# dK/dV as quarter-height row tiles, with fixed PSUM banks and a new step order, in a two-layer decode backward pass

## The chip, the cores and the metric

The kernel runs on one core of a Trainium2 chip. The metric is device time in microseconds (us). Each run of an experiment alternates with runs of the kernel before on the same chip. A ratio below is the mean time of one kernel's fast runs over the mean of the other's fast runs in the same rounds, so it is not quite the ratio of the medians quoted beside it. A run counts as fast when it is at most 1.5% above the fastest of the same kernel. Intervals are at 95%.

PE is the TensorE (matrix engine), PEld its weight loads, DVE and ACT the two engines that copy results out of PSUM (the banks into which the products are written), POOL the engine that issues the stores, SP the one that issues the loads. The granted clock is TensorE's clock as a share of full speed.

## The reference, cut to what matters

```python
# A: attention of one query token per batch over a cache, 32 query heads on 4 KV heads
q = (x @ wq) ...                        # B=2, D=1024, Hq=32, Hkv=4, Sk=16384, Dh=128
p = softmax(q k^T * Dh**-0.5); o = p v; A = o @ wo
# B: MLP with layernorm, gelu; D=1024, F=3584
x = x + A(ln(x)); x = x + B(ln(x)); x = x + A(ln(x)); x = x + B(ln(x))
# returned: the output, and the gradients of x, k_cache, v_cache, wq, wo, w1, b1, w2, b2
```

Both attention layers use the same caches. The gradients of K and V are therefore sums over two layers and eight query heads: for each of 8 groups (batch x KV head) and each cache row, 16 coefficients times 16 vectors of 128.

## The kernel before

The last stage walks through 32 chunks of 32 columns t (128 cache rows each), two "steps" of 16 columns per chunk. A step transposes V, makes the scores of dP, dS from them, accumulates dQ with K, makes dV and dK, and takes some "fill" units: the weight gradients, 512 columns each.

PSUM is shared out by pools; `px` is a pool of four banks for everything that is a matrix product here:

```python
ps_x = ctx.enter_context(tc.tile_pool(name="ps_x", bufs=4, space=PSUM))
def px(shape, dtype, name):
    return ps_x.tile(shape, dtype, name=name, tag="x")
```

dK/dV: for each of two t quads (a = 0 and 1), 64 coefficients (2 layers l x 8 heads x 4 t) against a block-diagonal matrix of 64 x (4 t x 128 d). Each quad is a row tile, half of the array's height:

```python
def kv_block(w, i, b):
    ...
    for a in range(2):
        ps = px([128, 4, 128], F32, "kv_ps")
        PE.matmul(ps[:]..., lhsT=blk[64 * a:64 * a + 64, b, :], rhs=Qm[64 * a:64 * a + 64, :, :]...,
                  start=True, stop=True, tile_position=(64 * a, 0))
        pss.append(ps)
    for a in range(2):
        evac_cast(sv_[:, b * 8 + a * 4:b * 8 + a * 4 + 4, :], pss[a][:], 512)
```

The backward product of Wq comes in four quarters. Its sum is kept in one tile of the same pool, from the first push of a quarter to the last:

```python
def quarter(kv):
    ...
    if j0 == 0 and j == 0:
        box["ps"] = px([128, DJ, 2], F32, "dn_b")           # one of the four banks, held
        V.memset(box["ps"][:], 0.0)
        box["pipe"] = BwdPipe(box["ps"], dq_all[:, hs, 0:2], True)
    ...
    box["pipe"].push(box["wv"], j, j0 + j, 0, 8)            # 8 transposes, a copy, 8 matmuls into dn_b
    if j0 + j == DJ - 1:
        box["pipe"].flush()
        V.tensor_tensor(out=dn_acc[:], in0=dn_acc[:], in1=box["ps"][:], op=ALU.add)
```

The step, cut to its order:

```python
while 2 * m < NS + 12 or late or fill:
    for s in (2 * m, 2 * m + 1):  kTs[s] = emit_T(cv, b, False)      # V transposes
    ... make_blk_V(i)                                                # on even m
    for s in (2 * m - 2, 2 * m - 1):  score0(s)
    kv_step(m, 0)                       # dV: 2 banks, dK: 2 banks
    sch.run_slot(1)                     # dQ accumulation
    ... make_blk_K(m // 2 - 2)
    step_fill((5 if m < 8 else 3) if m > 0 else 1)     # late (Wq) first, then the other weights
    kv_step(m, 1)                       # dV: 2 banks, dK: 2 banks
    m += 1
```

## Time and profile before

Median 1318.79 us of 3 runs (1310.5 to 1321.18); the profiled execution spans 1303.9 us.

These lines are from the page of the kernel before: busy time, share of the span and number of instructions of each engine, then the granted TensorE clock and the busy share of the DMA engines in 40 slices, in tenths.

```profile
PE 1108.1 (85%) x17053; PEld 801.8 (61%) x17053; DVE 631.0 (48%) x1320; ACT 573.0 (44%) x1407; POOL 63.5 (5%) x113
...
PEclk9998875879889589998998986795559657866655
DMA  9999999999999899999976827897779877978846
```

The last 17 slices look different from the rest: lower clock, DMA no longer full. The windows view puts numbers to it. Its columns are the stretch and its length in us, the busy us of PE, PEld, DVE, ACT and POOL with their instructions, the mean granted clock, the DMA share and GB/s. The stretches are: a piece of the first attention; all before the last stage; the last stage; its middle (60 us after its start to the last V transpose); and its tail.

```profile
60.00:140.00 80.00, 68.28 (x1209) 55.37 (x1206) 36.14 (x76) 35.18 (x156) 0.00 (x0) 0.91 1.01 425
0.00:757.70 757.70, 622.77 (x12528) 542.09 (x12528) 297.92 (x708) 263.85 (x837) 6.04 (x15) 0.86 0.95 383
757.70:1303.90 546.20, 485.35 (x4532) 259.72 (x4528) 333.09 (x612) 309.10 (x570) 57.48 (x98) 0.66 0.78 303
817.70:1230.30 412.60, 369.00 (x3569) 200.46 (x3567) 249.80 (x460) 233.20 (x432) 41.66 (x74) 0.67 0.85 330
1230.30:1303.90 73.60, 62.74 (x382) 27.13 (x379) 43.84 (x78) 39.31 (x70) 10.74 (x16) 0.57 0.57 235
```

For 757.7 us DMA is busy 0.95 of the time. The last stage takes 546.2 us; there no engine looks full but PE (485 us), and the clock is 0.66.

The next fence is the timeline of PE within one step of the stretch in which Wq's quarter is on its way (start, us, engine, line, operation, out<-in, shape, count, and in brackets PE's idle time before it and what ended it).

```profile
905.16 0.58 PE L831 MATMUL kv_ps<-QmK,blkK 64*128 64x512 bf16 x1 [0.25 <-ACT kv_stgV L150]
905.67 0.62 PE L338 MATMUL acc<-kv_K,dS_17826 128*32 128x512 bf16 x4
...
907.18 1.03 PE L245 MATMUL wtp<-ident,wqt 128*128 128x128 bf16 x8
908.01 0.40 PE L256 MATMUL dn_b<-dq_all,wT 128*128 128x2 bf16 x8
908.34 0.60 PE L734 MATMUL dw_ps<-rowsA,rowsB 4*128 4x512 bf16 x1
908.88 0.61 PE L831 MATMUL kv_ps<-QmV,blkV 64*128 64x512 bf16 x2
909.62 1.15 PE L831 MATMUL kv_ps<-QmK,blkK 64*128 64x512 bf16 x2
910.70 1.89 PE L317 MATMUL tp<-ident,kv_V 128*128 128x128 bf16 x16
912.38 0.62 PE L892 MATMUL dp<-doT_bf_16038,kT 128*128 128x8 bf16 x16
912.93 0.61 PE L831 MATMUL kv_ps<-QmV,blkV 64*128 64x512 bf16 x2
913.34 0.63 PE L831 MATMUL kv_ps<-QmK,blkK 64*128 64x512 bf16 x1
914.21 0.58 PE L831 MATMUL kv_ps<-QmK,blkK 64*128 64x512 bf16 x1 [0.25 <-ACT kv_stgV L150]
```

A step takes 9.05 us here (905.16 to 914.21). Two dK/dV matmuls of a pair that run side by side take 0.61 us together; the pair at 909.62 took 1.15, and at 913.34 and 914.21 the second one starts 0.87 us after the first: it waited for its bank to be copied out. The tile view of `dn_b` for this quarter (count, shortest/median/longest ns, first and last start):

```profile
L256 PE MATMUL dn_b<-dq_all,wT x64: 165/165/212, 898.4 to 956.4; 128*128 128x2 bf16 x64
L861 DVE MEMSET dn_b<- x1: 72/72/72, 889.8 to 889.8; 128x16 f32 x1
L870 DVE TENSOR_TENSOR dn_acc<-dn_acc,dn_b x1: 172/172/172, 956.6 to 956.6; 128x16 f32<-128x16 f32 x1
```

### The profile page before, as it was taken

Reading aid. Unit: us, or ns where it says so; the run is one execution under the profiler, and the core shown is the slowest. Engines: PE = TensorE matmul, PEld = TensorE weight load, DVE = VectorE, ACT = ScalarE, POOL = GpSimd, SP = SyncE. Lnnn points to the kernel's source line nnn. Section 1 sums busy time; section 2 is a strip of 40 time slices with the busy share of each in tenths; the row PEclk is TensorE's granted clock in tenths of the full one; section 3 lists DMA queues with packets and bytes.
Section 4 is the critical chain, followed back from the end, with each engine's and each line's share of the span. In section 5 each row is a group of like instructions: output and inputs, shape, how many; then the busy total and the mean of one; then the engine's idle time right before and its main releaser. Section 6 shows DMA issues by size and latency. Waiting matters only on the chain.

```text
span 1303.9 us, 38655 instructions
## 1 busy us (share of the span) xinstructions
PE 1108.1 (85%) x17053; PEld 801.8 (61%) x17053; DVE 631.0 (48%) x1320; ACT 573.0 (44%) x1407; POOL 63.5 (5%) x113
## 2 busy tenths in 40 slices
PE   4989874888988589878989989889998898898997
PEld 4867654876776579767789964445454545444442
DVE  1544421334444154433344556684457556655656
ACT  0544330234445024433333456674457455654655
POOL 0000000000000000000000001110011001000112
PEclk9998875879889589998998986795559657866655
DMA  9999999999999899999976827897779877978846
GB/s 379 423 425 424 424 417 395 347 397 426 419 424 399 320 396 343 424 424 425 425 271 230 309 99 260 334 410 284 282 282 415 350 304 311 408 271 317 325 195 257
DMA packets 86916, 455.51 MB, mean 349 GB/s; under 512 B 7122, under 2 KB 7122, under 8 KB 45788
## 3 DMA queue, kind: packets, MB, share of 16 engines
q1 hardware_dynamic: 69996, 354.46, 68.3%
q0 software_dynamic: 16752, 98.59, 18.7%
q8 instruction: 133, 2.18, 0.6%
q14 instruction: 35, 0.29, 0.1%
HBM read 354.44 MB, written 98.58 MB: 347 GB/s over the span
## 4 chain that ended last, share of the span: by engine, by line
PE 60%; DMA 24%; ACT 7%; DVE 6%; issue 2%; POOL 0%; SPq 0%; POOLq 0%; DVEq 0%; ACTq 0%
PE tp L317 15%; DMA kv_V<-in_A_v_cache_dram 13%; PE wtp L245 10%; PE kv_ps L831 7%; PE dw_ps L734 5%; PE acc L338 5%; DMA kv_K<-in_A_k_cache_dram 4%; DMA wt<-in_A_wo_dram 3%; ACT kv_stgV L150 2%; PE sc L452 2%; PE o_ps L349 2%; PE dp L892 2%; ACT dw_stg L150 2%; DMA wt<-in_B_w_dram 1%; DVE kT L145 1%
## 5 line engine op out<-in xcount | busy, mean ns | idle before, releaser
L142 ACT COPY kT<-tp 128x512 int32<-128x512 int32 x273 | 159.9, 586 | 343.7 <-PE tp L317 331.5
L145 DVE COPY kT<-tp 128x1024 bf16<-128x1024 bf16 x239 | 163.7, 690 | 210.7 <-PE tp L317 202.0
L317 PE MATMUL tp<-ident,kv_V 128*128 128x128 bf16 x2048 | 184.2, 253 | 12.4 <-DMA kv_V<-in_A_v_cache_dram 12.3
L317 PEld LDWEIGHTS <-kv_V 128*128 128x128 bf16 x2048 | 149.1, 115 | 60.1 <-issue 46.8
L317 PE MATMUL tp<-ident,kv_K 128*128 128x128 bf16 x2048 | 170.8, 232 | 5.1 <-DMA kv_K<-in_A_k_cache_dram 5.1
L245 PE MATMUL wtp<-ident,wt 128*128 128x128 bf16 x1664 | 137.9, 232 | 3.1 <-issue 1.7
L317 PEld LDWEIGHTS <-kv_K 128*128 128x128 bf16 x2048 | 129.1, 103 | 5.9 <-DMA kv_K<-in_A_k_cache_dram 5.7
L142 ACT COPY wT<-wtp 128x512 int32<-128x512 int32 x126 | 72.9, 579 | 136.1 <-PE wtp L245 116.4
L145 DVE COPY wT<-wtp 128x1024 bf16<-128x1024 bf16 x122 | 80.7, 665 | 105.3 <-PE wtp L245 104.8
L150 ACT CAST kv_stgV<-kv_ps 128x512 bf16<-128x512 f32 x164 | 92.7, 587 | 47.8 <-PE kv_ps L831 46.8
L831 PE MATMUL kv_ps<-QmK,blkK 64*128 64x512 bf16 x256 | 99.8, 502 | 15.1 <-ACT kv_stgV L150 4.9
L245 PEld LDWEIGHTS <-wt 128*128 128x128 bf16 x1664 | 106.2, 104 | 3.9 <-issue 2.4
L153 DVE CAST dw_stg<-dw_ps 128x512 bf16<-128x512 f32 x112 | 75.7, 688 | 40.4 <-PE dw_ps L734 39.3
L452 PEld LDWEIGHTS <-kT 128*128 128x128 bf16 x2048 | 76.7, 98 | 28.8 <-issue 21.2
L150 ACT CAST dw_stg<-dw_ps 128x512 bf16<-128x512 f32 x128 | 72.3, 591 | 43.8 <-PE dw_ps L734 42.7
L150 ACT CAST kv_stgK<-kv_ps 128x512 bf16<-128x512 f32 x137 | 80.2, 591 | 17.9 <-PE kv_ps L831 16.9
L153 DVE CAST kv_stgK<-kv_ps 128x512 bf16<-128x512 f32 x119 | 81.3, 685 | 12.5 <-PE kv_ps L831 10.1
L279 PEld LDWEIGHTS <-wt 128*128 128x128 bf16 x1920 | 54.3, 103 | 48.0 <-DMA wt<-in_A_wo_dram 14.0
L338 PE MATMUL acc<-kv_V,e_all 128*32 128x512 bf16 x512 | 56.3, 446 | 29.8 <-DMA kv_V<-in_A_v_cache_dram 24.7
L256 PEld LDWEIGHTS <-wT 128*128 128x128 bf16 x1920 | 77.2, 99 | 7.1 <-DVE wT L145 4.8
L153 DVE CAST kv_stgV<-kv_ps 128x512 bf16<-128x512 f32 x92 | 63.3, 688 | 35.9 <-PE kv_ps L831 35.1
L831 PE MATMUL kv_ps<-QmV,blkV 64*128 64x512 bf16 x256 | 75.8, 493 | 3.3 <-DVE dw_stg L153 1.0
(561 smaller groups left out, 1392.5 us busy)
## 6 DMA issues: line engine op xcount, KB each, us to landing
kv_K<-in_A_k_cache_dram SPq DMA_DIRECT2D x116, 1024.0 KB, 9.9
kv_V<-in_A_v_cache_dram SPq DMA_DIRECT2D x116, 1024.0 KB, 10.4
wt<-in_A_wo_dram SPq DMA_DIRECT2D x32, 1024.0 KB, 8.9
out_dram<-kv_stgV POOLq DMA_DIRECT2D x32, 1024.0 KB, 6.9
out_dram<-kv_stgK POOLq DMA_DIRECT2D x32, 1024.0 KB, 10.8
wt<-in_B_w_dram SPq DMA_DIRECT2D x32, 896.0 KB, 12.0
wt<-in_A_wq_dram SPq DMA_DIRECT2D x24, 1024.0 KB, 8.2
out_dram<-dw_stg POOLq DMA_DIRECT2D x23, 1024.0 KB, 5.4
```

The source lines that it names most:

```text
L142: S.copy(out=dst.bitcast(I32), in_=src.bitcast(I32))
L145: V.tensor_copy(out=dst, in_=src)
L150: S.copy(out=dst, in_=src)
L153: V.tensor_copy(out=dst, in_=src)
L245: PE.transpose(tp[:, o, :], wv[:, j, (o0 + o) * 128:(o0 + o + 1) * 128], ident[:])
L256: PE.matmul(self.out_ps[:, jj, :], lhsT=wT[:, o, :], rhs=self.gT[:, o0 + o, :], start=False, stop=True, skip_group_check=True)
L279: PE.matmul(fps[:, jo, :], lhsT=wv[:, j, jo * 128:(jo + 1) * 128], rhs=xT_bf[:, j0 + j, :], start=False, stop=True, skip_group_check=True)
L317: PE.transpose(tp[:, j, :], cv[:, b * 8 + j, :], ident[:])
L338: PE.matmul(self.acc[32 * cg:32 * cg + 32, :], lhsT=self.coef(b4), rhs=self.cv[:, q * 16 + cg * 4:q * 16 + cg * 4 + 4, :].rearrange("p t d ...
L452: PE.matmul(sc[g][f][:, :, t % TH], lhsT=kT[:, j, :], rhs=q_bf[:, g, :], start=True, stop=True)
L734: PE.matmul(ps[:], lhsT=xrows[p:p + 4, (j0 + j) * 128:(j0 + j + 1) * 128], rhs=yrows[p:p + 4, y0 + c0:y0 + c0 + 512], start=True, stop=Tru ...
L831: PE.matmul(ps[:].rearrange("p a b -> p (a b)"), lhsT=blk[64 * a:64 * a + 64, b, :], rhs=Qm[64 * a:64 * a + 64, :, :].rearrange("p a b -> ...
```

## The change

Its intent is to make the dK/dV products cheaper on TensorE and to take the waits for PSUM out of the last stage. Coefficients are laid out by t pair, not t quad, so 32 of them (2 layers x 8 heads x 2 t) form a row tile of a quarter of the array's height, and four run side by side. The same layout goes into the accumulations of O and dQ (128x16 weights against 256 columns, sixteen per chunk instead of eight). The four banks and the two transpose banks are fixed tiles in rotation; stores rotate over the eight tiles that held the last group's K and V; Wq's product of a push goes into any bank and is added to its sum at once; V's and K's coefficients are transposed and copied together; fill is four units per step, taken in turn from two queues.

```diff
-        pss = []
-        for a in range(2):
-            ps = px([128, 4, 128], F32, "kv_ps")
-            PE.matmul(ps[:]..., lhsT=blk[64 * a:64 * a + 64, b, :], rhs=Qm[64 * a:64 * a + 64, :, :]...,
-                      start=True, stop=True, tile_position=(64 * a, 0))
+        pss = [mx() for _ in range(4)]
+        for b in range(2):
+            for r in range(4):
+                PE.matmul(pss[r][:, b * 256:(b + 1) * 256], lhsT=blk[32 * r:32 * r + 32, o + 2 * h + b, :],
+                          rhs=Qm[32 * r:32 * r + 32, :, :]..., start=True, stop=True, tile_position=(32 * r, 0))
+        for r in range(4):
+            evac_cast(sv_[:, 2 * h:2 * h + 2, r], pss[r][:]..., 512)
...
-                        box["ps"] = px([128, DJ, 2], F32, "dn_b")
+        def product(wT, j):
+            ps = mx()
+            for o in range(8):
+                PE.matmul(ps[:, 0:2], lhsT=wT[:, o, :], rhs=dq_all[:, kv * 8 + o, 0:2], start=(o == 0), stop=(o == 7))
+            V.tensor_tensor(out=dn_acc[:, j, :], in0=dn_acc[:, j, :], in1=ps[:, 0:2], op=ALU.add)
...
     def step_fill(n):
-        for _ in range(n):
-            if late: late.popleft()()
-            elif fill: fill.popleft()()
+        for k in range(n):
+            for q in ((late, fill) if k % 2 == 0 else (fill, late)):
+                if q and q[0].ready():
+                    q.popleft()()
+                    break
...
+        for k in range(2):                  # the step: one slot, then the other
+            s = 2 * m + k
+            ... transposes of slot s; score0(s - 2)
+            if k == 1 and late_pe: late_pe.popleft()()          # Wq
+            ... make_blks(m // 2, m // 2 - 2)                   # V and K coefficients together
+            kv_step("KV"[k], m, (5, 1)[k])                      # four banks
         sch.run_slot(1)
-        step_fill((5 if m < 8 else 3) if m > 0 else 1)
-        kv_step(m, 1)
+        step_fill((5 if m < 8 else 4) if m > 0 else 1)
```

## The prediction

> **What bounds it now.** The windows view cuts the kernel in two. Up to about 755 us it reads caches and weights: DMA share 0.95, TensorE clock 0.86. DMA binds, and little should change there. From 755 to 1304 us (549 us) dK/dV and the weight gradients are made: DMA share only 0.78, PE busy 488 of 549 us, DVE 334, ACT 310, granted clock 0.66. So TensorE, at half clock much of the time, binds this stage. Inside it the timeline shows two regimes. At full clock (975 to 1005 us: clock 0.95, DMA share 1.01) a step of two slots takes about 5.4 us, DMA-bound. While Wq's backward runs (889 to 982 us: clock 0.54) a step takes about 9 us, and the TensorE is busy 86 of 93 us. The last 54 us are mostly weight-gradient work (clock 0.50, DMA share 0.53).
>
> **What the change does there.**
> - dK/dV products: 512 matmuls 64x512, two row tiles at once, become 1024 of 32x256, four at once. Before's pairs start together (timeline). Per step the streamed time halves: four pairs of about 0.43 us at half clock become half of that, so -0.85 us (-0.43 us at full clock). The Trainium skill, "TensorE: Matmul & The Clock Gate", Part 3, measures 3.07x for four 32-row tiles, so most of it should arrive.
> - Waits for PSUM: in a 9 us step the dK/dV products take 3.6 us from start to next start, against 1.7 us of streaming. One of the four rotating banks is held by Wq's accumulator for a whole quarter. The change frees it and spaces the uses four at a time between transposes. I expect -0.5 to -1 us.
> - dK coefficients: 16 small transposes per chunk become 4, and two 128x512 copies become one 128x1024: -0.1 us per step.
> - Fill: four units a step, not three, alternating between jobs in different row tiles, so their matmuls overlap. The tail mostly vanishes (-25 to -35 us); per step +0.6 us of evictions and 0.13 MB of stores.
> - Acc: twice as many matmuls, half as wide, half-width eviction: neutral.
>
> **Floor.** The stage moves 303 GB/s x 549 us = 166 MB; at the 424 GB/s seen earlier that is 392 us. Evictions are about 15 per step at 0.64 us on two engines, plus 0.9 us of DVE work: about 5.3 us a step. TensorE at half clock needs about 6 us. Three limits near 6 us do not overlap perfectly: I take 6.5 us x 65 steps = 423 us, plus 45 us of start and end = 468 us. Saving about 80 us in the profile (1304 to about 1222). The skill's same page, Part 4, says transposes do not count as busy for the clock; so fewer products may leave the clock at half, which is why I don't take the whole way to the floor.
>
> **Prediction:** 1225 us, 8 in 10 within 1170 to 1275; faster by over 2% 0.93, within 2% 0.05, slower 0.02.
>
> **What would show it.** Right: the stage after 755 us shrinks to 430 to 500 us with DMA share above 0.85; the dK/dV matmuls start four at once; Wq steps fall from 9 to below 7.5 us; the tail falls below 30 us; the first 755 us stay within 10 us. Wrong: steps stay at 9 us with PE waiting for DVE/ACT evictions (four banks asked for at once), or the granted clock falls below 0.6 and eats the saving, or stores wait for homes (DMA waits in front of dK/dV evictions), or the first stage grows through the doubled accumulation matmuls. If the clock rises to 0.8 or more, the stage reaches its DMA floor and the time goes to about 1160 us.

## More of the kernel before

From 889.8 to 956.6 us one of the four banks holds sixteen numbers per partition. In that stretch the clock is at half throughout:

```profile
889.00:957.00 68.00, 62.74 (x517) 32.28 (x516) 32.96 (x56) 31.24 (x56) 5.02 (x9) 0.50 0.73 273
```

PE counts as busy for 62.74 of 68 us, and that reading is treacherous: a matmul that is slow because of the clock counts as busy in full. Over this whole profile a dK/dV matmul takes 604 ns (median) at half clock and 372 ns at full clock.

## The result, and the profile after

Median 1224.06 us of 3 runs (1223.42 to 1226.32) against 1318.79 us; the ratio is 0.93 (0.9233 to 0.9366). The profiled execution spans 1222.2 us.

The page's busy line, and the windows of the kernel after, cut as for before:

```profile
PE 1016.8 (83%) x18045; PEld 784.8 (64%) x18045; DVE 612.2 (50%) x1298; ACT 558.7 (46%) x1396; POOL 76.8 (6%) x145
```

```profile
60.00:140.00 80.00, 63.75 (x1267) 52.00 (x1267) 34.05 (x71) 32.87 (x153) 0.00 (x0) 0.92 1.01 419
0.00:766.90 766.90, 613.59 (x13198) 537.86 (x13199) 295.77 (x710) 261.21 (x836) 6.82 (x17) 0.86 0.95 379
766.90:1222.20 455.30, 403.23 (x4853) 246.92 (x4850) 316.45 (x588) 297.50 (x560) 69.95 (x128) 0.65 0.90 362
826.90:1175.00 348.10, 319.64 (x3897) 197.95 (x3897) 253.95 (x463) 241.79 (x456) 59.69 (x110) 0.64 1.00 405
1175.00:1222.20 47.20, 32.91 (x290) 16.59 (x287) 22.29 (x51) 17.81 (x34) 4.47 (x8) 0.54 0.67 271
```

The last stage is 90.9 us shorter (546.2 to 455.3): 64.5 us in its middle, 26.4 us in its tail. The middle is now at DMA share 1.00. The clock is not higher (0.65 against 0.66). The first stage is 9.2 us longer, and its reads run at 419, not 425 GB/s. 90.9 - 9.2 = 81.7 us is the difference of the spans.

The timeline of PE shows the quarter-height products of one half step of the kernel after:

```profile
986.28 0.41 PE L922 MATMUL dp<-doT_bf_16728,kT 128*128 128x8 bf16 x8
986.62 0.39 PE L858 MATMUL xm_16741<-QmK,blk 32*128 32x256 bf16 x1
986.62 0.39 PE L858 MATMUL xm_16738<-QmK,blk 32*128 32x256 bf16 x1
986.63 0.39 PE L858 MATMUL xm_16739<-QmK,blk 32*128 32x256 bf16 x1
986.63 0.39 PE L858 MATMUL xm_16740<-QmK,blk 32*128 32x256 bf16 x1
986.81 0.42 PE L858 MATMUL xm_16741<-QmK,blk 32*128 32x256 bf16 x1
...
987.17 1.03 PE L988 MATMUL tpm_16743<-ident,kv_V 128*128 128x128 bf16 x8
```

The four start within 0.01 us of each other, the next four 0.19 us later, and the next transposes start 0.55 us after the group does (986.62 to 987.17). By the picture alone, the row tiles do what they are meant to do, and the total lies 1 us from the forecast.

### The profile page after: what moved, and what is told of

It reads as the page before. It is cut to its first block, busy times and chain, and to the rows that moved or that the text cites. A ratio compares the mean times of both kernels' runs of the same rounds, so it can differ in the third digit from the quotient of the medians.

```text
span 1222.2 us, 40886 instructions
## 1 busy us (share of the span) xinstructions
PE 1016.8 (83%) x18045; PEld 784.8 (64%) x18045; DVE 612.2 (50%) x1298; ACT 558.7 (46%) x1396; POOL 76.8 (6%) x145
## 5 line engine op out<-in xcount | busy, mean ns | idle before, releaser
L144 ACT COPY kT<-tp 128x512 int32<-128x512 int32 x200 | 117.5, 588 | 286.0 <-PE tp L316 276.3
L144 ACT COPY wT<-wtp 128x512 int32<-128x512 int32 (+1 forms) x109 | 63.2, 580 | 122.1 <-PE wtp L247 112.6
L147 DVE COPY wT<-wtp 128x1024 bf16<-128x1024 bf16 (+1 forms) x107 | 70.3, 659 | 91.8 <-PE wtp L247 88.0
L452 PEld LDWEIGHTS <-kT 128*128 128x128 bf16 x2048 | 76.3, 98 | 27.3 <-issue 20.5
L316 PE MATMUL tp<-ident,kv_V 128*128 128x128 bf16 x896 | 74.4, 231 | 9.7 <-DMA kv_V<-in_A_v_cache_dram 8.9
L416 ACT ACTIVATE e_all<-sc,negm 128x64 bf16<-128x64 f32 x256 | 77.2, 345 | 1.4 <-DVE negm L411 1.4
L336 PE MATMUL acc_all<-kv_V,e_all 128*16 128x256 bf16 x896 | 47.2, 290 | 27.0 <-DMA kv_V<-in_A_v_cache_dram 24.8
L416 ACT ACTIVATION_READ_ACCUMULATOR e_all<-sc,negm 128x1 f32 x256 | 60.3, 236 | 0.0
L988 PE MATMUL tpm_16742<-ident,kv_V 128*128 128x128 bf16 x448 | 50.9, 283 | 0.0
L988 PE MATMUL tpm_16743<-ident,kv_V 128*128 128x128 bf16 x448 | 49.6, 278 | 0.0
L922 PE MATMUL dp<-doT_bf_16728,kT 128*128 128x8 bf16 x1024 | 49.5, 176 | 0.0
L922 PEld LDWEIGHTS <-kT 128*128 128x128 bf16 x1024 | 48.2, 109 | 0.4 <-issue 0.4
```

Source lines behind the costliest of these rows:

```text
L144: S.copy(out=dst.bitcast(I32), in_=src.bitcast(I32))
L147: V.tensor_copy(out=dst, in_=src)
L316: PE.transpose(tp[:, j, :], cv[:, b * 8 + j, :], ident[:])
L336: PE.matmul(ACCT[cg:cg + 16, 0:256], lhsT=self.coef(u), rhs=self.cv[:, t:t + 2, :].rearrange("p t d -> p (t d)"), start=(u < 4), stop=(u > ...
L416: S.activation(out=e_all[:, g, f * half:(f + 1) * half, l, h, :], in_=sc[g][f][:, h, :].rearrange("p (a b) -> p a b", b=2), func=ACT.Exp, ...
L452: PE.matmul(sc[g][f][:, :, t % TH], lhsT=kT[:, j, :], rhs=q_bf[:, g, :], start=True, stop=True)
```

## The experiments

Three theories. R: TensorE's streaming at half clock bound the last stage, and halving it is the main gain. B: waits for PSUM banks bound it, above all the bank held for Wq. S: the gain comes from the fill rate and the shorter tail. Names with `a_` start from the kernel after, with `b_` from the kernel before. All runs gave correct results.

| run | what differs | median us | before us | ratio (95%) |
|---|---|---|---|---|
| a_half | after, 64-row tiles | 1214.53 | 1305.09 | 0.9314 (0.9265 to 0.9363) |
| a_fill3 | after, three fill units | 1227.92 | 1305.09 | 0.9404 (0.9339 to 0.9469) |
| b_fill4 | before, four fill units | 1310.46 | 1305.09 | 1.0023 (0.9954 to 1.0092) |
| b_bank | before, bank freed | 1263.98 | 1305.09 | 0.9692 (0.9636 to 0.9749) |
| a_again | after, unchanged | 1229.16 | 1310.77 | 0.938 (0.935 to 0.9411) |
| a_pad | after, 64 bytes of padding | 1218.21 | 1310.77 | 0.9301 (0.9264 to 0.9338) |
| a_hold | a_half, bank held again | 1283.96 | 1310.77 | 0.9791 (0.9755 to 0.9827) |
| b_bank4 | b_bank, four fill units | 1272.76 | 1310.77 | 0.9699 (0.9654 to 0.9745) |
| b_space4 | b_bank4, step order of after | 1231.23 | 1307.74 | 0.9443 (0.9394 to 0.9492) |
| a_halfpad | a_half and a_pad | 1206.63 | 1307.74 | 0.9242 (0.92 to 0.9283) |
| a_best | a_halfpad, last Wq quarter transposed ahead | 1211.8 | 1307.74 | 0.9294 (0.926 to 0.9328) |
| a_halfold | a_halfpad, fill queues as before | 1208.02 | 1306.35 | 0.9248 (0.9201 to 0.9295) |

Runs with equal "before" values shared a call.

### a_half: are the row tiles the gain?

```diff
-                PE.matmul(pss[r][:, b * 256:(b + 1) * 256], lhsT=blk[32 * r:32 * r + 32, ...], rhs=Qm[32 * r:32 * r + 32]...)
+                PE.matmul(pss[2 * b + a][:], lhsT=blk[64 * a:64 * a + 64, ...], rhs=Qm[64 * a:64 * a + 64]...)   # Qm is 4 x 128 wide
```

> The kernel after, with only the dK/dV products put back to 64-row tiles (512 matmuls of 64x512, two at once) and their stationary operand widened to match; coefficients by t pair, bank and home rotation, order and fill stay. Theory R (row tiles: TensorE streaming at half clock was what bound the last stage, so halving it is the main gain): the products cost 0.85 us more per step at half clock, 0.43 us at full clock, over 64 steps, so 30 to 55 us come back, 1255 to 1280 us. Theory S (scheduling: bank rotation, spacing, fill, tail): under 12 us come back, at most 1236 us.

It took 1214.53 us, ratio 0.9314: with tiles of half the height, and twice the streaming, the whole gain is still there. Theory R falls for the kernel after, where the middle of the stage is at its DMA rate with either tile. No run puts quarter tiles alone into the kernel before, so what they would have been worth there, with the bank still held, is not shown. Windows of its last stage, whole and middle:

```profile
770.50:1217.50 447.00, 379.05 (x4370) 213.09 (x4366) 315.71 (x591) 295.66 (x557) 69.99 (x128) 0.80 0.90 368
830.50:1172.00 341.50, 296.14 (x3508) 165.44 (x3507) 255.08 (x468) 242.06 (x457) 59.89 (x110) 0.83 1.01 413
```

PE is busy for less time than with quarter tiles (379.05 against 403.23 us), although its tiles stream twice the columns; the clock is 0.80 and not 0.65. The clock records of both have the values 0.5 and 1.0 alone, as the Trainium skill says ("TensorE: Matmul & The Clock Gate", Part 1: two states, set by how busy the array has been). In the last stage they give half clock for 176 of 447.0 us with 64-row tiles, and 323 of 455.3 us with 32-row tiles. What the quarter tiles saved in columns they lost in clock. That the form of the dK/dV products is the cause is shown, since the edit changes only them, their operand and the order in which their results are copied out. That it acts by a lower activity of the array is the page's mechanism, and fits, but no run measures the activity itself.

The prediction said that at a clock of 0.8 or more the time would go to about 1160 us. Here the clock is 0.80 and it does not: the stage takes 447.0 us, with its middle at DMA share 1.01.

### b_bank and a_hold: the held bank

b_bank gives the kernel before what `product` of the change does, and nothing else:

```diff
-                        box["ps"] = px([128, DJ, 2], F32, "dn_b")      # held through a quarter
+            ps = px([128, 2], F32, "dn_b")                             # one push, then
+            V.tensor_tensor(out=dn_acc[:, jj, :], in0=dn_acc[:, jj, :], in1=ps[:], op=ALU.add)
```

> The kernel before, with Wq's product given a bank per push and added to its sum by DVE, so that no PSUM bank is held through a quarter. If the held bank was what made the dK/dV products wait in the 9 us steps (3.6 us from start to start for 1.7 us of streaming), those steps fall to 8 to 8.5 us, 32 of them, 16 to 32 us faster than before. If the waits come from two evictions engines being behind whatever the number of banks: within 8 us of before.

The ratio is 0.9692, beyond the range that even the theory of the bank gave. The window of b_bank is a Wq stretch like the one shown of before, then the whole last stage:

```profile
898.00:958.00 60.00, 53.61 (x628) 31.24 (x616) 38.78 (x76) 36.14 (x69) 5.33 (x10) 0.76 0.88 342
760.90:1262.30 501.40, 444.49 (x4532) 246.35 (x4528) 332.82 (x636) 307.02 (x570) 57.67 (x98) 0.72 0.84 330
```

The matmuls are the same in number (x4532). In the first Wq quarter the pushes start 9.33 us apart before (888.97 to 954.30 us, seven gaps) and 6.50 us apart here (899.23 to 944.75), and the clock there is 0.76, not 0.50. So the low clock before was in good part a result of the waits, not their cause. The gain also lies where the bank was held: over the three quarters of Wq that fall among the steps, the pushes span 183.8 us before and 136.8 us in b_bank, 47.0 us less, and the last stage is 44.8 us shorter.

a_hold does the opposite. It takes a_half, holds bank 3 for Wq's sum while a quarter is on its way, and lets the rest rotate over three (dK/dV go two and two, since four banks are no longer there):

```diff
-        return nxt("x", X)
+        return nxt("x", X[:3] if late_pe else X)
...
-            ps = mx()
+            ps = X[3][:, 0:2 * DJ]...        # added to dn_acc once, after the last push
```

> The kernel after with 64-row tiles (as a_half), and Wq's sum again held in one of the four banks while a quarter of Wq is on the way, the other uses rotating over three. Theory B (the held bank was the main loss before): 25 to 45 us slower than a_half's 0.931 of before, 0.95 to 0.966. Rival (order and spacing alone make up for it): below 0.940.

It gave 0.9791: of the 0.0686 that a_half gains, 0.0477 is lost, about 62 us, more than expected. Over the same three quarters its pushes span 211.6 us, a_half's 142.3: 69.3 us more, where its last stage is 68.3 us longer. Theory B is confirmed from both sides. Its last stage:

```profile
768.50:1283.80 515.30, 458.27 (x4373) 237.38 (x4370) 320.37 (x563) 301.34 (x557) 69.97 (x128) 0.66 0.82 319
```

The clock is back at 0.66, at nearly the same number of matmuls as a_half (x4373 and x4370).

The Trainium skill says that consistent bubbles can mean there is too little PSUM for the next tile ("Perfetto Trace Analysis", Optimization Strategy). The bracket [0.25 <-ACT kv_stgV L150] recurs at 905.16 and 914.21, one step apart. But the brackets alone undersize it; most of the cost is hidden in matmuls that count as busy.

### b_fill4, b_bank4, a_fill3: fill rate and tail

```diff
-        step_fill((5 if m < 8 else 3) if m > 0 else 1)
+        step_fill((5 if m < 8 else 4) if m > 0 else 1)      # b_fill4; b_bank4 with b_bank; a_fill3 the reverse
```

> The kernel before, with four fill units per step instead of three. Theory S: the tail of 54 us mostly goes, 25 to 40 us faster than before. Theory R: the steps lengthen by nearly what the tail loses, since TensorE at half clock binds them: within 12 us of before.

> The kernel before with the freed bank and four fill units. b_fill4 alone gave nothing, b_bank alone 0.969. If the missing fill rate counts only once the bank is free (the steps then have room, the tail of 73 us after the last V transposes goes to about 48): 12 to 25 us faster than b_bank, 0.950 to 0.960. If the stage is by then bound by bytes or by waits that need the new spacing: within 8 us of b_bank.

> The kernel after, with three fill units per step instead of four (60 instead of about none of the weight-gradient matmuls fall after the last V transposes). Theory D (the stage is now at its DMA rate, 420 GB/s from 820 to 1190 us): steps get shorter by about what they no longer store, the same bytes move later, a tail with idle DMA of 10 to 20 us appears, 1230 to 1245 us. Theory S: the fill rate and the missing tail are the main gain: 1255 us or more. Theory R alone: about 1224 to 1235 us.

b_fill4 is 1.0023 of before, b_bank4 0.9699 against b_bank's 0.9692, a_fill3 0.9404 where a_again has 0.938. The fill rate is worth nothing measurable in any of the three. (b_fill4's profile fell in a slower execution and is not used.) Theory S, as far as fill goes, falls: the tail of 73.6 us before is cut to 47.2 us after, but the same evictions and stores then stand in the steps. So it is in b_bank4 against b_bank: the tail falls from 73.5 to 51.5 us, and the middle grows from 367.9 to 395.8 us (here the latter):

```profile
823.30:1219.10 395.80, 351.55 (x3652) 198.14 (x3650) 266.43 (x501) 245.00 (x462) 46.87 (x80) 0.72 0.92 359
```

b_bank4 missed its expectation of a further 12 to 25 us; a_fill3, expected at 1230 to 1245 us, came out just below, at 1227.92.

### b_space4: the order of the step

```diff
-        for s in (2 * m, 2 * m + 1):  ... emit_T ...       # both slots
-        for s in (2 * m - 2, 2 * m - 1):  ... score0 ...
-        kv_step(m, 0) ; run_slot ; step_fill ; kv_step(m, 1)
+        for k in range(2):  emit_T(2m+k) ; score0(2m+k-2) ; kv_step(m, k)
+        run_slot ; step_fill
```

> b_bank4 with one thing more: the step's order is that of the kernel after (transposes of a slot, its scores, then one group of dK/dV products, twice; then accumulation and fill), so that no two groups of bank users stand next to each other but the fill. b_bank4 was 0.970 of before, the kernel after 0.938 with the same 64-byte offset undone 0.930. Theory B2 (banks: a group of four evictions needs TensorE work without a bank beside it): 0.935 to 0.950, DMA share in the middle of the stage from 0.92 to 0.97 or more. Rival (the rest comes from the merged coefficient transposes, alternating fill, quarter tiles): 0.962 or more.

The ratio goes from 0.9699 to 0.9443, as the theory of banks said. Middle of its last stage, with 64-row tiles and every other part of before:

```profile
821.00:1176.90 355.90, 325.49 (x3656) 186.49 (x3656) 260.00 (x491) 240.40 (x469) 46.58 (x80) 0.76 0.97 394
```

The DMA share there is 0.97, where b_bank4 had 0.92 (its middle: 395.8 us). Order alone, with no instruction taken away, brought the stage nearly to its DMA rate. That it acts through the banks shows in the pairs of dK/dV matmuls: in the middle of the stage the second starts over 0.1 us after the first in 101 of 214 pairs before, in 64 of 214 in b_bank4, and in 31 of 214 here. A group of bank users did better with work beside it that uses none.

### a_again and a_pad: the slower reads

The profiles of the kernel before and of its variants show 425 GB/s from 60 to 140 us, the kernel after and a_half 419. By the memory map of the compiled programs, the load buffers are at address 74496 before (a multiple of 256) and at 74432 after (64 below). a_pad adds 64 bytes:

```diff
+    pad = const.tile([128, 16], F32, name="pad")
+    V.memset(pad[:], 0.0)
```

> The kernel after, unchanged, as the control for the others of this call: ratio 0.925 to 0.937 to before; first stage again at 418 to 420 GB/s, where all kernels of the before family showed 425.

> The kernel after with 64 bytes of padding among the constants, so that the load buffers start at the same SBUF address as before (74496, a multiple of 256) and not 64 bytes lower. Theory A (the start address of the load buffers sets the DMA rate): the first stage goes back to 424 to 426 GB/s and ends 7 to 11 us earlier, 0.991 to 0.995 of a_again. Rival (the slower reads come from the doubled accumulation matmuls, or from the narrower writes of exp): rate stays at 418 to 420, time within 3 us of a_again.

a_pad took 1218.21 us, a_again 1229.16 us in the same rounds: 0.991. (a_again's 0.938 lies just outside its expected 0.925 to 0.937.) The window 60 to 140 us, of a_again and then of a_pad:

```profile
60.00:140.00 80.00, 64.73 (x1272) 53.09 (x1272) 34.26 (x72) 33.25 (x154) 0.00 (x0) 0.90 1.01 418
```

```profile
60.00:140.00 80.00, 67.68 (x1297) 54.98 (x1290) 34.75 (x73) 34.08 (x155) 0.00 (x0) 0.87 1.01 424
```

The DMA share is 1.01 in both: DMA is as busy, and moves less. The last stage starts at 765.6 us in a_again and at 758.9 us in a_pad. (a_pad's profiled execution was its slowest, 1228.25 us; the others lie between 1214.87 and 1222.07.) So the 64 bytes are the cause; they move everything allocated behind them, and that it is the load buffers that matter is likely but not separated. The Trainium skill has a possible reason ("DMA: Bandwidth & Descriptors", How a descriptor splits into AXI transactions): a transaction that reads must start at a 256-byte boundary, and a descriptor that does not begin there costs extra beats. The page says this of reads, while here the shifted address is the one that the loads write to. If its rule held for that side too, a run of 8192 bytes that starts 192 past a boundary would need 262 beats instead of 256, an estimate of 2.3%; measured is 1.4%. No run shows the beats.

### a_halfpad, a_best, a_halfold: a better version, and what is left

> 64-row tiles (a_half) and the 64-byte padding (a_pad) together. The two are independent (the first stage gains 7 to 11 us from the reads; the last stage is at its DMA rate either way): 0.922 to 0.929 of before; a_pad with quarter tiles was 0.930. Granted clock of the last stage about 0.80 against 0.62 with quarter tiles.

a_halfpad is 0.9242 of before, the fastest of all, 1206.63 us; a_pad, the same with quarter tiles, had 0.9301. Its last stage and the middle of it:

```profile
758.20:1204.60 446.40, 376.19 (x4372) 213.20 (x4368) 315.78 (x591) 295.22 (x557) 69.82 (x128) 0.81 0.90 369
818.20:1160.50 342.30, 294.06 (x3496) 166.36 (x3495) 254.18 (x466) 240.89 (x455) 59.74 (x110) 0.84 1.00 411
```

a_best tried to shorten the tail by transposing the last Wq quarter before its dQ is there, into the space of e_all of groups already done:

```diff
+        if len(ready) == G - 2:
+            make_ahead(HKV - 2)      # load, 8 x 8 transposes, copies into e_all[:, 0:2] and e_all[:, 4:6]
```

> a_halfpad, and for the last quarter of Wq the transposes are made ahead, into the space of coefficients no longer needed, since they don't wait for dQ; after dQ only the products are left. The tail from the last V transposes to the end is 45.5 us in a_half, of which about 24 us are nine steps of transpose, copy, product one after the other: 10 to 15 us less, 0.912 to 0.921 of before. If the tail is bound by its stores instead: no change from a_halfpad.

It was slower, 0.9294, where 0.912 to 0.921 was expected. Its middle is 7.4 us longer than a_halfpad's (349.7 against 342.3 us) at the same DMA share of 1.00. Two lines of its PE timeline show what became of the tail:

```profile
1174.57 1.04 PE L939 MATMUL tpm<-ident,wqt 128*128 128x128 bf16 x8 [1.67 <-DMA wqt<-in_A_wq_dram]
1179.50 0.60 PE L338 MATMUL acc_all<-kv_K,dX 128*16 128x256 bf16 x8 [3.89 <-DMA kv_K<-in_A_k_cache_dram]
```

The loads of Wq now stand before the last loads of K in a stretch where DMA is full, and PE waits for both. The quarter's two loads of 1 MB alone take about 5 us at the middle's 410 GB/s (an estimate). The tail is shorter by 2.0 us only (42.1 against 44.1).

a_halfold puts the fill queues back (Wq's work first, no taking in turn):

```diff
-            for q in ((late, fill) if k % 2 == 0 else (fill, late)):
+            for q in (late, fill):        # and Wq's pushes as units of late
```

> a_halfpad with the fill taken as before: the late queue first, Wq's transposes and products as units in it, no alternation, four units per step. b_space4 (0.944) and a_halfpad (0.924) still differ by 2%: if that is the alternation and the separate place of Wq's transposes, this run gives 0.934 to 0.945; if it is the merged coefficient transposes and copies and the fixed homes, 0.922 to 0.930.

0.9248: the alternation is worth nothing measurable. What still separates b_space4 (0.9443) from a_halfpad (0.9242) are the merged coefficient transposes and copies, the fixed tiles, the homes and the half-size accumulators. They were not told apart; that stays open.

## Why the prediction was right or wrong, point by point

- **The total** was right: 1225 forecast, 1224.06 measured, but by luck, as the next points show. So were the size of the last stage (468 forecast, 455.3 measured), its steps (6.5 us forecast; (1175.0 - 766.9)/64 = 6.4 us), and the DMA share above 0.85 (0.90). The pushes of the first Wq quarter came 6.6 us apart (46.0 us for seven gaps), below the 7.5 forecast.
- **"TensorE, at half clock much of the time, binds this stage."** Only on the surface. b_bank has the same matmuls and is 41 us faster; the low clock and the busy PE were in good part made by waits for a bank. The floor has it too, as one of three limits near 6 us a step. But a_half and a_halfpad, at clock 0.80 and 0.81, take 447.0 and 446.4 us for the stage, little less than the 455.3 at 0.65, and the middle of all three is at DMA share 1.00 or 1.01: there DMA was the limit that bound.
- **"-0.85 us (-0.43 us at full clock)" for the row tiles, "so most of it should arrive".** This is the term that failed. The four tiles do start at once, but a_half, without them, is as fast (0.9314 against 0.93 and 0.938), and a_halfpad is if anything faster than a_pad (0.9242 against 0.9301, in different calls, their intervals overlapping). Beside the other parts of the change it should have stood at zero or slightly above.
- **"-0.5 to -1 us" for the waits for PSUM.** The mechanism was right, the size too small. The held bank alone was worth 2.8 us in each step of the first Wq quarter (9.33 to 6.50) and about 2 us in the next two, 41 us by b_bank and about 62 us by a_hold; the spacing another 0.0256 of the time (b_bank4 to b_space4), about 33 us. Spread over 64 steps that is 1.2 to 1.5 us, an estimate from these runs. One term too large and one too small roughly cancel; that is how the total came out, and it was luck.
- **Tail "-25 to -35 us"**: 26.4 us, right, but it was paid back in the steps, as b_fill4, b_bank4 and a_fill3 show. (The prediction counts its tail from a later point, 54 us before and not 73.6, so its "below 30 us" cannot be held against the 47.2 us here.)
- **Acc "neutral"** and **dK coefficients "-0.1 us"**: no run separates them.
- **"Fewer products may leave the clock at half"**, taken from Part 4 of the same page of the Trainium skill (transposes don't count as busy in the same way): borne out as far as the clock goes. It stayed at 0.65, and 64-row tiles raised it to 0.80. The reason given for it is not: in the profile before, from 739.2 to 757.0 us, TensorE did only transposes (217 recorded) and products against two columns (232), and the granted clock was 1.00 throughout. That speaks against the page, though no run has transposes by themselves.
- **First stage "within 10 us"**: it grew by 9.2 us, inside the limit, most of it (6.7 us between a_again and a_pad) for a reason not foreseen, the 64 bytes.
- **"If the clock rises to 0.8 or more ... about 1160 us"**: wrong. a_half has 0.80 and takes 1214.53 us, a_halfpad 0.81 and 1206.63 us.

## What to carry to other kernels

An accumulator that keeps one of few rotating PSUM banks for a long stretch can cost far more than its few matmuls show: here 41 to 62 us, which appeared as busy PE and as a low clock, and which small adds of its own took away. Halving the columns that TensorE streams was worth nothing here, in a stage where the clock fell with it and DMA was full; and order (no two groups of bank users side by side) was worth 2.6% with no instruction taken away. A forecast whose total fits is not yet an explanation: undo each part alone. And look at where the large buffers start after every change of the constants.

## What the Trainium skill lacked or had wrong

- "TensorE: Matmul & The Clock Gate", Part 3, gives the speed-up of packed row tiles (3.07x for four) without what it does to the clock. Here 32-row tiles left the last stage at half clock for 323 of 455.3 us, 64-row tiles for 176 of 447.0 us, and the time did not fall.
- The same page, Part 1, names two ways to lose the clock: idle gaps over about 3.4 us, and short idle times while PSUM banks are cycled, by which the clock swings between its states. It does not measure what waits for a bank cost the clock of a whole stage. Here it was 0.50 throughout from 889 to 957 us with PE recorded busy for 62.74 of 68 us and no gap over 0.67 us; freeing one bank raised it to 0.76 in the same quarter of Wq.
- "DMA: Bandwidth & Descriptors", How a descriptor splits into AXI transactions, gives the rule for reads that do not start at a multiple of 256 bytes, but nothing on the side that is written, and no measured cost. Here, with load buffers 64 bytes below such a multiple, reads ran at 418 to 419 GB/s instead of 424 to 425, 1.4%, and the kernel took 0.9% longer (a_again against a_pad).
- "Perfetto Trace Analysis", Optimization Strategy, names consistent bubbles as a possible sign of too little SBUF or PSUM, but not that the cost can sit in recorded busy time. Here the recurring gap was 0.25 us in a step of 9 us, and the missing bank cost 2.8 us of it.
